# A fused attention and two-MLP kernel: every SBUF tile behind the constants moved up by 288 bytes

## The chip, the core and the metric

One core of one Trainium2 chip runs the whole kernel as a single program. The metric is device time in microseconds (us), the median of several runs. The profile is of one execution of the same program, with its own time.

## The reference

```
attention:  phi(x) = exp(x*scale @ omega.T - |x*scale|^2/2 - max) / sqrt(m)     q, k, v: [4, 8, 576, 64], 128 features
            out = phi(q) @ (phi(k).T @ v) / (phi(q) . sum(phi(k)) + 1e-6)       -> x [2304, 512]
first MLP:  h = x @ w_in [512, 2048];  g = h * sigmoid(1.702 h);  x = g @ w_out [2048, 512]
second MLP: 8 experts, one per token (argmax of x @ w_gate), weighted by the softmax of the gate:
            y = relu(x @ w1[e] [512, 1024]) @ w2[e] [1024, 512]
```

All inputs and outputs are float32.

## The kernel before

There are three stages, and TensorE works through them in one order that is written out by hand (no scheduler reorders anything).

**Attention** runs over 18 tiles of 128 tokens. Plain float32 matmuls project keys and queries (L228), sum keys against values (L254), transpose (L280, L305) and divide (L290). While it runs, VectorE and ScalarE decode the first MLP's weights and split each into a high part and a low part. The low parts go to DRAM (L155) and come back one 128x512 tile at a time (`wfetch` L369, `ofetch` L375).

**The first MLP** runs over five blocks of tokens, three of 512 and two of 384, and in each over 16 slices of 128 hidden features. For one block and slice, `hmm` (L436, L437, L438) makes 12 matmuls: for each of four contraction chunks high weight times high x, high weight times low x, low weight times high x. `gate` (L451 to L453) applies the gate and splits the result into `gh` and `gl`. `ymm` (L462, L463, L465) makes 12 matmuls more (9 in a block of 384). So a step is 24 matmuls of 512 columns, or 12 of 384 and 9 of 512. All operands are of type float32r, 4 bytes an element. Every matmul has a weight load (LDWEIGHTS) of its own, of a 128x128 operand, and TensorE loads the weights of the next matmul while the present one streams its moving operand.

**The second MLP** runs over 8 blocks of 288 gathered tokens of one expert each: `ffn1` (L802, L803, L806) and `ffn2` (L818, L819, L821), 12 matmuls of 288 columns each per 128 hidden features. The results are transposed back (L838) and scattered to DRAM (L845).

**Where the operands lie.** The tile framework places tiles in each SBUF partition from two sides. From the low side come the pools `keep` (its first tile is `cst`, the constants), `wts`, and the left pools of attention and of routing. From the top come the right pools `xa` and `xb`, which hold x's halves `xh` and `xl`, `gh`, `gl`, `sg` and one buffer of the second MLP's weights, `wh0`. The constants take 524 float32 a partition (2,096 bytes, L78), and what follows them starts where they end. The built program gives every tile's byte address. Modulo 512 they are, before the change:

| operands | role | address modulo 512 |
|---|---|---|
| `xh`, `xl` (right side) | moving in L436 to L438 | 480 |
| `win`, `l0` (left side) | weights in L436 to L438 | 192 |
| `wo`, `l1` (left side) | moving in L462, L463, L465 | 192 |
| `gh`, `gl` (right side) | weights in L462, L463, L465; moving in L818, L819, L821 | 480 |
| `yhl` (left side), chunk k = 0 to 3 | moving in L802, L803, L806 | 192, 320, 448, 64 |
| `wh0` (right side); `l0` (left side) | weights in L802, L803; in L806 | 480; 192 |
| `wh1`, `l1` (left side) | weights in L818 and L821; in L819 | 192 |
| `cst` (first tile of `keep`) | identity in the transposes | 128 |

So in the first MLP moving operand and weights lie 288 or 224 bytes apart modulo 512, that is, 224 bytes one way or the other. Where TensorE goes from one group to the next inside a step, two pairs agree: the weights `gh` of the first L462 are loaded while the last L438 streams `xh` (480 and 480), and the weights `win` of the next step's first L436 are loaded while the last L465 streams `wo` (192 and 192). In `ffn1` the four chunks of `yhl` lie at four addresses modulo 512: against `wh0` the distances are 224, 352, 480 and 96, against `l0` 0, 128, 256 and 384. In `ffn2` the distance is 288 throughout.

Of the kernel before, what the change touches and what calls it, by code (L numbers as in the profile page):

```python
# [10 lines left out]
F32 = mybir.dt.float32  # L11
# [37 lines left out]
NCONST = C_E8 + 8  # L49
# [21 lines left out]
def fused_kernel(ctx: ExitStack, tc: tile.TileContext, qT, kT, vt, omT, w_in, w_out, w_gate, w_gateT, w1, w2, consts, out):  # L71
    nc = tc.nc
    ctx.enter_context(tc.manual_schedule())
    keep = ctx.enter_context(tc.tile_pool(name="keep", bufs=1))
    drp = ctx.enter_context(tc.tile_pool(name="dr", bufs=1, space=DRAM))
    wts = ctx.enter_context(tc.tile_pool(name="wts", bufs=1))

    cst = keep.tile([128, NCONST], F32, name="cst")  # L78
    ident = cst[:, C_ID:C_ID + 128]
    xT = [keep.tile([128, KC, nb * 128], F32, name=f"big{i}", tag=f"big{i}") for i, (_, nb) in enumerate(BLOCKS)]  # L80
    win = [wts.tile([128, 4, KC, 128], F32R, name=f"win{i}", tag=f"win{i}") for i in range(4)]
# [234 lines left out]
    def advance():  # L316
        if ln[0] < len(seq):
            load(*seq[ln[0]])
        if 2 <= ln[0] < len(seq) + 2:
            square(*seq[ln[0] - 2])  # L320
        ln[0] += 1
# [13 lines left out]
    for t in range(3):  # L335
        if t >= 2:
            cload(1)
        advance()
    nc.sync.dma_start(out=cst, in_=consts)


    wg = []
# [345 lines left out]
    for n in range(len(steps) + 1):  # L688
        if n < len(steps):
# [52 lines left out]
            if (b, f) == (0, HF):  # L742
                assert cnext[4] == len(order)
                for i in range(2):
                    wg.append(keep.tile([128, 4, DM], F32, name=f"wg{i}", tag=f"wg{i}", bufs=1))
                    nc.sync.dma_start(out=wg[i].rearrange("p e d -> p (e d)"),
                                      in_=w_gate[4 * i:4 * i + 4].rearrange("(o e) d -> o (e d)", o=1).to_broadcast([128, 4 * DM]))
# [337 lines left out]
```

## Time and profile before

| | |
|---|---|
| median of 3 runs | 809.25 us (808.79 to 810.22) |
| the profiled execution's own time | 809.69 us |
| its span, first to last instruction | 807.9 us |
| TensorE matmul busy | 782.8 us, 97% of the span, 5681 instructions |
| VectorE, ScalarE, GpSimd busy | 483.5, 372.9 and 157.7 us |
| hardware DMA queue | 50.8% of 16 engines' span, 124.04 MB |

A busy share is the time in which at least one instruction of that engine was under way, divided by the span. Matmuls are pipelined: one of 512 columns is shown for 0.40 us, but the next one starts 0.23 us after it. What a matmul costs in a stream is therefore read from the starts of successive matmuls, not from their durations. The time outside the span (809.69 less 807.9) is 1.8 us.

### The profile page before, as it was taken

How to read it: one execution, taken by the hardware profiler on the slowest of the kernel's cores; microseconds unless marked ns; L12 is line 12 of the kernel's file. 1: busy time of each engine (PE TensorE's matmuls, PEld its weight loads, DVE VectorE, ACT ScalarE, POOL GpSimd, SP SyncE). 2: the span in 40 equal slices, each digit the busy share in tenths (PEclk: the TensorE clock that was granted, in tenths of full speed). 3: DMA queues.
4: the chain of work that ended last, by engine and by line, in shares of the span. 5: the costliest groups of instructions: out<-in, count | busy, mean ns of one | idle time of the engine just before them, and what ended most of it. 6: DMA issues, size and time to landing. Idle time of an engine off the chain costs nothing.

```text
span 807.9 us, 15072 instructions
## 1 busy us (share of the span) xinstructions
PE 782.8 (97%) x5681; PEld 700.5 (87%) x5681; DVE 483.5 (60%) x1075; ACT 372.9 (46%) x873; POOL 157.7 (20%) x129
## 2 busy tenths in 40 slices
PE   8999999799999999999999999999999999999994
PEld 7899998577888888888789988988999999999993
DVE  3688878679655137765315844744787556556551
ACT  5788889545433222212122123224454655555551
POOL 3656646100000111100020011100015502311011
PEclk9999999899999999999999999999999999999997
DMA  9877654389874473543335445974066646554011
GB/s 213 204 164 161 152 136 141 116 257 313 292 247 152 135 247 106 158 129 92 91 93 169 130 128 157 340 264 158 12 247 220 220 161 222 188 214 138 27 30 34
DMA packets 66016, 134.55 MB, mean 167 GB/s; under 512 B 24784, under 2 KB 24848, under 8 KB 61584
## 3 DMA queue, kind: packets, MB, share of 16 engines
q1 hardware_dynamic: 62784, 124.04, 50.8%
q0 software_dynamic: 3072, 9.44, 3.9%
q8 instruction: 47, 0.77, 0.4%
q14 instruction: 33, 0.27, 0.1%
q10 hardware_dynamic: 80, 0.03, 0.0%
HBM read 118.81 MB, written 18.87 MB: 170 GB/s over the span
## 4 chain that ended last, share of the span: by engine, by line
PE 58%; issue 23%; POOL 6%; DVE 5%; DMA 3%; ACT 2%; SPq 0%; POOLq 0%; ACTq 0%; DVEq 0%
PE py L462 8%; PE py L465 8%; PE py L463 8%; PE ph L436 7%; PE ph L437 7%; PE ph L438 7%; PE pj L228 6%; POOL out L845 2%; POOL yg L630 2%; PE kv L254 2%; PE nu L290 2%; PE tr L280 1%; DMA raw<-qT 1%; PE xt L305 1%; ACT phiq L237 1%
## 5 line engine op out<-in xcount | busy, mean ns | idle before, releaser
L451 ACT ACTIVATE gh<-ph 128x512 fp32r<-128x512 f32 (+1 forms) x80 | 44.5, 556 | 240.1 <-PE ph L438 240.1
L453 DVE TENSOR_TENSOR gl<-sg,gh 128x512 fp32r<-128x512 f32 (+1 forms) x80 | 51.1, 639 | 168.1 <-ACT sg L452 161.4
L438 PE MATMUL ph<-xh,l 128*128 128x512 f32 (+1 forms) x320 | 119.2, 373 | 1.0 <-DMA l<-lod 1.0
L436 PE MATMUL ph<-xh,win 128*128 128x512 f32 (+1 forms) x320 | 120.0, 375 | 0.0
L462 PE MATMUL py<-wo,gh 128*128 128x512 f32 x288 | 114.8, 399 | 4.6 <-ACT big L306 4.6
L437 PE MATMUL ph<-xl,win 128*128 128x512 f32 (+1 forms) x320 | 119.2, 372 | 0.2 <-DVE xl L178 0.2
L463 PE MATMUL py<-l,gh 128*128 128x512 f32 x288 | 114.8, 399 | 0.0
L497 DVE CUSTOM_DVE_ANT_0 junk<-ysb,wg 128x512 f32<-128x512 f32 x120 | 87.0, 725 | 3.1
L178 POOL TENSOR_TENSOR xl<-big,xh 128x512 fp32r<-128x512 f32 (+1 forms) x20 | 24.4, 1221 | 325.4 <-ACT xh L177 266.2
L465 PE MATMUL py<-wo,gl 128*128 128x512 f32 x288 | 81.0, 399 | 0.0
L228 PE MATMUL pj<-omx,raw 128*128 128x128 f32 x576 | 74.1, 284 | 2.1 <-DVE raw L213 1.5
L228 PEld LDWEIGHTS pj<-omx,raw 128*128 128x128 f32 x576 | 69.0, 197 | 4.4 <-issue 2.4
L213 POOL TENSOR_TENSOR raw<-raw 64x1024 f32<-64x1024 f32 (+1 forms) x34 | 65.0, 1916 | 37.1 <-DMA raw<-kT 14.2
L818 PE MATMUL oT<-gh,wh 128*128 128x288 f32 x256 | 72.1, 304 | 0.0
L802 PE MATMUL ph<-yhl,wh 128*128 128x288 f32 x256 | 72.0, 304 | 0.0
L819 PE MATMUL oT<-gh,l 128*128 128x288 f32 x256 | 70.1, 294 | 0.0
L803 PE MATMUL ph<-yhl,wh 128*128 128x288 f32 x256 | 69.9, 295 | 0.0
L437 PEld LDWEIGHTS ph<-xl,win 128*128 128x128 f32 x320 | 60.2, 188 | 10.5 <-DVE xl L178 0.6
L438 PEld LDWEIGHTS ph<-xh,l 128*128 128x128 f32 x320 | 60.1, 188 | 10.4 <-DMA l<-lod 1.9
L462 PEld LDWEIGHTS py<-wo,gh 128*128 128x128 f32 x288 | 54.6, 190 | 16.6 <-ACT big L306 4.9
L436 PEld LDWEIGHTS ph<-xh,win 128*128 128x128 f32 x320 | 60.2, 188 | 9.8
L235 DVE TENSOR_REDUCE nm<-pj 128x4 f32<-128x512 f32 x72 | 48.5, 688 | 30.6 <-PE pj L228 24.9
(178 smaller groups left out, 1437.9 us busy)
## 6 DMA issues: line engine op xcount, KB each, us to landing
l<-lod SPq DMA_DIRECT2D x160, 256.0 KB, 3.1
f<-w SPq DMA_DIRECT2D x20, 1024.0 KB, 6.3
e<-w SPq DMA_DIRECT2D x16, 1024.0 KB, 6.1
st<-w_in SPq DMA_DIRECT2D x16, 512.0 KB, 4.7
st<-w_out SPq DMA_DIRECT2D x16, 512.0 KB, 4.6
lod<-l SPq DMA_DIRECT2D x32, 256.0 KB, 3.5
yd<-ysb SPq DMA_DIRECT2D x22, 256.0 KB, 2.7
raw<-kT SPq DMA_DIRECT2D x18, 256.0 KB, 3.8
```

Of the source, the lines that this page charges most:

```text
L228: nc.tensor.matmul(p[:, j], r[:, 4 * g + j], omx, start=True, stop=True)
L436: nc.tensor.matmul(p, wh[:, c], xh, start=k == 0, stop=False)
L437: nc.tensor.matmul(p, wh[:, c], xl, start=False, stop=False)
L438: nc.tensor.matmul(p, wl[:, c], xh, start=False, stop=k == KC - 1)
L462: nc.tensor.matmul(p, gh[:, c], wh, start=(b, f) in pfirst, stop=False)
L463: nc.tensor.matmul(p, gh[:, c], wl, start=False, stop=False)
L465: nc.tensor.matmul(p, gl[:, j * 128:(j + 1) * 128], wh, start=False, stop=(b, f) in plast)
L497: nc.vector.tensor_tensor_reduce(out=junk, in0=ysb[b][j], in1=wg[e // 4][:, e % 4], scale=1.0, scalar=0.0, op0=ALU.mult, op1=ALU.add, accu ...
L802: nc.tensor.matmul(p, wh[:, w], yh[:, k], start=k == 0, stop=False)
L803: nc.tensor.matmul(p, wh[:, w], yl[:, k], start=False, stop=False)
L818: nc.tensor.matmul(p, wh[:, w], hh, start=f == 0, stop=False)
L819: nc.tensor.matmul(p, wl[:, w], hh, start=False, stop=False)
```

## The change

```diff
-    cst = keep.tile([128, NCONST], F32, name="cst")
+
+    cst = keep.tile([128, NCONST + 72], F32, name="cst")
...
-    nc.sync.dma_start(out=cst, in_=consts)
+    nc.sync.dma_start(out=cst[:, 0:NCONST], in_=consts)
```

The constants' tile gets 72 unused columns of 4 bytes, 288 bytes a partition. The tile itself stays where it is, and its load writes the same 2,096 bytes of each partition. Every tile that is placed from the low side behind it moves up by 288 bytes; the tiles of the right side stay. No instruction is added, removed or moved on any engine, and no wait or semaphore differs. Only addresses do (and, with the blank line, line numbers by one). Modulo 512, after the change:

| operands | address modulo 512 | distance, moving to weights |
|---|---|---|
| `xh`, `xl`, `gh`, `gl`, `win`, `l0`, `wo`, `l1` | 480 | 0 in L436 to L438 and in L462, L463, L465 |
| `yhl`, chunk k = 0 to 3 | 480, 96, 224, 352 | 0, 128, 256, 384 in L802, L803 and L806 |
| `wh1`, `l1` against `gh`, `gl` | 480 | 0 in L818, L819, L821 |
| operands of L228, L254 and L290 | as before to each other | as before |
| `cst` | 128 | differs by 288 against everything that it is used with from the low side |

288 is 4.5 times 64: tiles of the low side that began at a multiple of 64 bytes now begin 32 bytes past one.

## Rows read from the trace of the kernel before

**Rows 1.** The page: span, part 1 and the granted clock in 40 slices.
```profile
span 807.9 us, 15072 instructions
PE 782.8 (97%) x5681; PEld 700.5 (87%) x5681; DVE 483.5 (60%) x1075; ACT 372.9 (46%) x873; POOL 157.7 (20%) x129
PEclk9999999899999999999999999999999999999997
```
**Rows 2.** Busy time in the stages: first MLP, blocks of 512; of 384; the second MLP.
```profile
163.87:423.52 259.65, 258.45 (x1108) 206.71 (x1107) 143.53 (x308) 83.26 (x151) 14.82 (x12) 1.00 0.57 178
423.52:560.48 136.96, 136.96 (x706) 123.23 (x705) 76.43 (x231) 34.80 (x78) 7.85 (x8) 1.00 0.60 189
560.48:807.90 247.42, 233.38 (x1819) 230.83 (x1817) 145.49 (x318) 126.18 (x257) 51.33 (x48) 0.98 0.42 146
```
**Rows 3.** Waits of PE: waiter, released by: us in total, times, longest.
```profile
PE py L462 <- ACT big L306: 4.6, 1, 4.6
...
PE ph L438 <- DMA l<-lod: 1.0, 2, 0.8
```
**Rows 4.** Windows of PE alone: us, busy (matmuls touched), granted clock, DMA share, GB/s.
```profile
158.75:163.44 4.69, 4.69 (x12) 0.50 0.62 190
272.03:328.03 56.00, 56.00 (x241) 1.00 0.49 154
...
432.57:449.34 16.77, 16.77 (x85) 1.00 0.55 169
```
**Rows 5.** Lines by form: first-MLP and second-MLP matmuls, counts, durations of one.
```profile
L462 PE MATMUL py<-wo,gh 128*128 128x512 f32 x288 | 114.8, 399 | 4.6 <-ACT big L306 4.6
...
L436 PE MATMUL ph<-xh,win 128*128 128x512 f32 x192 | 76.2, 397 | 0.0
...
L818 PE MATMUL oT<-gh,wh 128*128 128x288 f32 x256 | 72.1, 304 | 0.0
...
L436 PE MATMUL ph<-xh,win 128*128 128x384 f32 x128 | 43.7, 342 | 0.0
```
**Rows 6.** Timeline of PE in one first-MLP step: start us, duration us, instruction.
```profile
274.60 0.39 PE L438 MATMUL ph<-xh,l 128*128 128x512 f32 x1
274.83 0.40 PE L462 MATMUL py<-wo,gh 128*128 128x512 f32 x1
275.06 0.40 PE L463 MATMUL py<-l,gh 128*128 128x512 f32 x1
...
277.39 0.40 PE L465 MATMUL py<-wo,gl 128*128 128x512 f32 x1
277.63 0.39 PE L436 MATMUL ph<-xh,win 128*128 128x512 f32 x1
277.86 0.40 PE L437 MATMUL ph<-xl,win 128*128 128x512 f32 x1
```
**Rows 7.** Timeline of PE in the second MLP: starts of an `ffn2` and an `ffn1` group.
```profile
655.40 0.29 PE L818 MATMUL oT<-gh,wh 128*128 128x288 f32 x1
...
657.00 0.30 PE L802 MATMUL ph<-yhl,wh 128*128 128x288 f32 x1
...
658.07 0.69 PE L806 MATMUL ph<-yhl,l 128*128 128x288 f32 x4
658.59 0.29 PE L818 MATMUL oT<-gh,wh 128*128 128x288 f32 x1
```
**Rows 8.** Lines L178 and L838: engine, operation, count, duration ns min/median/max, first and last start.
```profile
L178 DVE TENSOR_TENSOR l<-e,wh x64: 679/691/695, 555.7 to 759.7; 128x512 fp32r<-128x512 f32 x64
...
L838 PE MATMUL ob<-cst,oTs x96: 270/272/314, 617.1 to 796.2; 128*96 128x128 f32 x96
```
**Rows 9.** DMA issues: queue, count, KB each, median us from issue to landing.
```profile
raw<-kT SPq DMA_DIRECT2D x18, 256.0 KB, 3.8
v<-vt SPq DMA_DIRECT2D x18, 256.0 KB, 4.5
```
**Rows 10.** The chain that ended last: shares by engine.
```profile
PE 58%; issue 23%; POOL 6%; DVE 5%; DMA 3%; ACT 2%; SPq 0%; POOLq 0%; ACTq 0%; DVEq 0%
```

## The prediction

> **What bounds the kernel now.** I read the page first. TensorE is busy for 97% of the span, at the full clock in all but a few slices [rows 1], so first of all the time is what TensorE streams. The stage table says where this holds without a gap: in the first MLP's blocks of 512 it is busy for 258.45 of 259.65 us, in its blocks of 384 for all of 136.96, and in the second MLP for 233.38 of 247.42 [rows 2]. The reader should see that a nanosecond on each matmul of the first MLP is a nanosecond on the end, because nothing else ends last there: the longest waits of TensorE on others are one of 4.6 us on a ScalarE copy and 1.0 us in all on reloaded low weights [rows 3]. The chain of waits gives PE 58% and "issue" 23%, the latter mostly time behind TensorE's own pipelined stream; DMA has 3% [rows 10].
>
> Next I read what one matmul costs. Ten steps of 24 matmuls of 512 columns take 56.00 us, 240 starts after one another: 0.2333 us each [rows 4]. The same matmuls at half clock (granted clock 0.50) take 4.69 us for eleven, 0.4264 each [rows 4]. Half of that is 0.2132. So at full clock, and there alone, each matmul takes 0.0201 us more than its columns, some 9%. This excess is the only thing that an address could take away or add to, and the change is worth what it does to it.
>
> **The change part by part.** No instruction, wait or order changes on any engine, so nothing moves past anything else in a queue, and no new wait arises. Four kinds of address change are left.
>
> *Operands of the first MLP.* From 224 bytes apart modulo 512 to 0. The counts are 3 times 192 plus 3 times 288, so 1,440 matmuls of 512 columns, and 3 times 128, so 384 of 384 columns [rows 5]. How does TensorE do where the two agree already? Twice in each step they do. The last L438 streams from an address that agrees with the weights `gh` loaded meanwhile, and the next matmul starts 0.23 us later (274.60 to 274.83); the last L465 agrees with the next `win`, and the next starts 0.24 us later (277.39 to 277.63) [rows 6]. Together that is 0.47 us for two, where two ordinary ones take 0.4667. One is a little under the mean, one a little over, both within the rounding of the starts. From this I take 0 for the change. The two ends are every matmul at 0.23 or every one at 0.24. At 0.23: 1,440 times 0.0033 is 4.8 us, and 384 at three quarters of it 0.95, together a gain of 5.7 us. At 0.24: 1,440 times 0.0067 is 9.6 and 384 at three quarters 1.9, a loss of 11.5 us.
>
> Two more readings speak for 0. If the excess came from weight loads that collide with the stream, it would be one amount per matmul, since each loads the same 128x128 operand. Four steps of the blocks of 384 take 16.77 us [rows 4]; less 36 matmuls at 0.2333 (8.40) that leaves 8.37 for 48, 0.1744 each, against 0.1599 for the columns (three quarters of 0.2132): an excess of 0.0145, not 0.0201. In the second MLP twelve matmuls of 288 columns take 1.60 us in `ffn2` and 1.59 in `ffn1` [rows 7], so 0.1333 and 0.1325 against 0.1199: an excess of 0.013. It falls with the columns that are streamed, so most of it belongs to the stream itself and not to a meeting with the weights. Proportion would give 0.0113 at 288; what is over that, under 0.002 a matmul, is all that looks like a fixed piece per load.
>
> And `ffn1` is a trial of addresses made already: its chunks meet their weights at distances 0, 96, 128, 224, 256, 352, 384 and 480 modulo 512, `ffn2` at 288 alone. If the distance mattered, the two groups would differ by more than 1.59 against 1.60 [rows 7].
>
> The Trainium skill's page "TensorE: Matmul & The Clock Gate" (Part 2, "Step-by-step: what each phase is for") says that TensorE reads weights and moving operand through two independent SBUF ports, so that loading the next weights takes no read bandwidth from the running matmul. By it the change is worth 0 wherever the operands lie, and the two agreeing pairs of rows 6 go with it.
>
> *Operands of the second MLP.* `ffn2` goes from 288 to 0, `ffn1` from its eight distances to four (0, 128, 256, 384). 0 by the same reading; at the ends 768 matmuls of `ffn2` could gain the whole 0.0134 each, 10.3 us, which only the large rival below would bring, or lose in proportion to the first MLP's.
>
> *Transposes and attention.* The attention's matmuls keep their distances. The transposes use `cst`, which stays while the rest moves. L838 does so already with weights at four addresses modulo 512, and its shortest and median durations are 270 and 272 ns [rows 8]: 0.
>
> *VectorE, ScalarE, GpSimd and DMA.* Low-side tiles now start 32 bytes past a multiple of 64. VectorE's L178 reads its second operand alternately from `wh0` (480, such an address) and `wh1` (192, a multiple of 64), and all 64 last 679 to 695 ns [rows 8]: 0, and these engines have room. For DMA the trace shows no transfer of long rows to such an address. The nearest rows are the loads of k (rows of 4,096 bytes that begin on 64) with 3.8 us, and of v (pieces of 256 bytes every 260, most of which do not) with 4.5 us for the same 256 KB [rows 9], and that difference may be due to the short pieces alone. Lower end 0, since no start becomes a rounder one; upper end all DMA on the chain 18% longer: 3% of 807.9 is 24.2 us [rows 10], so 4.4 us. I take 0: in the MLPs TensorE waits on reloads for 1.0 us in all [rows 3], and what hides the rest is the matmul stream. If that cover went, L438 would be late first, on its low weights.
>
> **Sum.** 0 on the profiled execution's own time of 809.69 us, which is 0.44 above the median of 809.25. Carried to the median: **809.2 us**. The runs of before spread over 1.4 us, so about 0.2% is what can be told from no change.
>
> **The rivals.**
> 1. *The whole excess is a bank or line meeting of the two streams, and agreement removes it.* For it: the excess appears at full clock alone, as a limit of reading would. Against it: rows 6 and 7, where agreeing pairs and mixed distances show no gain. Price: 1,440 times 0.0201 is 28.9 us, and 384 times 0.0145 is 5.6; together 34.5, so about 775 us. `ffn2` would make it 765.
> 2. *A small part goes.* The agreeing L438 pair is the pattern (0.23), or the fixed piece under 0.002 us. Price 5.7 us at most: 803.5 us.
> 3. *Agreement costs.* When every weight load begins on the same line as the stream that it runs beside, the two meet at once in each matmul, and the L465 pair is the pattern (0.24 [rows 6]). It decides as soon as the mean start distance in a step exceeds 0.2345 us or so, 0.5% over now; at 0.24 it costs 11.5 us: 820.8 us. Against it: the other pair is under the mean, and the chunk at distance 0 in `ffn1` sits in the shorter group.
>
> That the change doesn't do what it says is no rival: the addresses in the built program are the stated ones.
>
> To rival 1, the same page (Part 1, "Wait — 56ns, not 53.3ns?") gives 512 columns at full clock as 512/2.4 plus 2.5 ns, 215.8 ns. The trace has 233.3 [rows 4]. By that figure 17.5 ns on 1,440 matmuls, 25.2 us, would be there to win, an estimate of 784 us; the page does not say what the rest is.
>
> **How the numbers follow.** No change 0.57, rival 1 0.11, rival 2 0.14, rival 3 0.18. So faster by over 0.2% 0.25, within it 0.57, slower 0.18. The range takes in the forecast, rival 2 to its end (803.5), the DMA bound (813.6) and the lower half of rival 3, to 815. Left out are rival 1 (0.11) and the upper half of rival 3 (0.09).
>
> **What would show it.** In the profile after, ten steps like those of rows 4 should again take 56.0 us, an `ffn2` group 1.60 and an `ffn1` group 1.59, and the PE row of the page should stay near 782.8 us. Rival 1 shows as steps of about 5.1 us in place of 5.60, rival 2 as 5.52, rival 3 as 5.64 to 5.76. A later start of the matmuls on low weights (the wait of L438 growing past a few us, or raw and l landing later) would show the DMA bound. The prediction is wrong if the steps differ from 5.60 by more than 0.02 us, or if a stage loses time in waits that rows 3 does not list.

## The result, and the profile after

| | before | changed |
|---|---|---|
| median | 809.44 us (808.79 to 810.22, 4 runs) | 802.31 us (800.25 to 803.71, 4 runs) |
| profiled execution, its span | 809.69, 807.9 us | 802.9, 801.0 us |
| TensorE matmul busy | 782.8 us | 774.5 us |

The ratio is 0.9909 [0.9885, 0.9934]: 7.1 us or 0.9% faster, more than the 0.2% that can be told from no change. The forecast was 809.2 us with no change likeliest; the time lies 1.2 us under the lower end of its range. Line numbers of the changed kernel are one higher, so L437 to L439 are the matmuls into `ph`, L463, L464 and L466 those into `py`.

The page of the changed kernel (span, part 1, granted clock), against [rows 1]:

```profile
span 801.0 us, 15072 instructions
PE 774.5 (97%) x5681; PEld 699.8 (87%) x5681; DVE 484.0 (60%) x1075; ACT 372.3 (46%) x873; POOL 157.8 (20%) x129
...
PEclk9999999999999999999999999999999999999997
```

The same instructions, the same granted clock but for one slice, the other engines' busy times unchanged within 0.6 us, and 8.3 us less matmul time. The waits of PE (waiter, releaser: us, times, longest) that [rows 3] names are there again:

```profile
PE py L463 <- ACT big L307: 4.6, 1, 4.6
...
PE ph L439 <- DMA l<-lod: 1.7, 2, 1.3
```

So neither wait went away; the one on low weights even grew by 0.7 us. The gain is in the stream itself. Windows of PE alone (us, busy with matmuls touched, clock, DMA share, GB/s) show it: ten steps of 24 matmuls of 512 columns, four steps in the blocks of 384, then the stages from the first `ph` matmul to the first one of 384 columns, from there to the second MLP, and the second MLP to its last L839. In the changed kernel:

```profile
275.85:330.25 54.40, 54.40 (x241) 1.00 0.50 165
426.68:443.42 16.74, 16.74 (x85) 1.00 0.56 167
146.78:417.62 270.84, 264.00 (x1183) 0.99 0.57 181
417.62:556.12 138.50, 138.50 (x713) 1.00 0.59 191
556.12:789.50 233.38, 231.00 (x1810) 0.99 0.43 149
```

And the same three stages before:

```profile
145.58:423.52 277.94, 271.97 (x1183) 0.99 0.57 176
423.52:562.30 138.78, 138.78 (x713) 1.00 0.60 191
562.30:796.20 233.90, 231.30 (x1811) 1.00 0.43 148
```

Ten steps take 54.40 us where they took 56.00 [rows 4], 5.440 a step for 5.600. That is 0.2267 a matmul for 0.2333, so each gained 0.0067 us, a third of the 0.0201 that each took beyond its columns. Were all 48 steps of the blocks of 512 to gain as much, it would be 48 times 0.160, 7.68 us. Their stage is 7.10 us shorter: busy time fell by 7.97 and time not busy rose by 0.87, of which 0.7 is the wait of L439. The blocks of 384, from which the prediction's bounds expected a third of any gain (0.95 us by their 384 matmuls of 384 columns and 0.95 by the 288 of 512 between them, of 5.7), are only 0.28 us shorter, and the second MLP 0.5 us. Up to the first `ph` matmul the profiled execution of the change lost 1.2 us (146.78 against 145.58). That is scatter: the further kernels below start there between 144.8 and 146.4, and the changed kernel, profiled again, at 145.3.

The timeline of PE in one step of the changed kernel (start us, duration us, instruction) is to be read beside [rows 6]:

```profile
273.13 0.39 PE L463 MATMUL py<-wo,gh 128*128 128x512 f32 x1
273.36 0.39 PE L464 MATMUL py<-l,gh 128*128 128x512 f32 x1
273.58 0.39 PE L463 MATMUL py<-wo,gh 128*128 128x512 f32 x1
...
274.94 1.07 PE L466 MATMUL py<-wo,gl 128*128 128x512 f32 x4
275.85 0.39 PE L437 MATMUL ph<-xh,win 128*128 128x512 f32 x1
```

The printed starts move by 0.23 and 0.22: a gap of 0.2267 and one of 0.2333 can both be printed as 0.23. Only a run of many matmuls tells the two apart.

### The profile page after: what moved, and what is told of

Read it like the earlier page. It is cut to its first block, busy times and chain, and to the rows that moved or that the text cites. A ratio compares the mean times of both kernels' runs of the same rounds, so it can differ in the third digit from the quotient of the medians.

```text
span 801.0 us, 15072 instructions
## 1 busy us (share of the span) xinstructions
PE 774.5 (97%) x5681; PEld 699.8 (87%) x5681; DVE 484.0 (60%) x1075; ACT 372.3 (46%) x873; POOL 157.8 (20%) x129
## 4 chain that ended last, share of the span: by engine, by line
PE 59%; issue 23%; POOL 6%; DVE 3%; DMA 3%; ACT 2%; SPq 1%; POOLq 0%; ACTq 0%; DVEq 0%
PE py L463 8%; PE py L464 8%; PE py L466 8%; PE ph L437 7%; PE ph L438 7%; PE ph L439 7%; PE pj L229 6%; POOL out L846 2%; POOL yg L631 2%; PE kv L255 2%; DMA lod<-l 2%; PE nu L291 2%; PE tr L281 1%; DMA raw<-kT 1%; PE xt L306 1%
## 5 line engine op out<-in xcount | busy, mean ns | idle before, releaser
L439 PE MATMUL ph<-xh,l 128*128 128x512 f32 (+1 forms) x320 | 118.1, 369 | 1.7 <-DMA l<-lod 1.7
L437 PE MATMUL ph<-xh,win 128*128 128x512 f32 (+1 forms) x320 | 118.8, 371 | 0.0
L438 PE MATMUL ph<-xl,win 128*128 128x512 f32 (+1 forms) x320 | 117.8, 368 | 0.3 <-DVE xl L179 0.3
L463 PE MATMUL py<-wo,gh 128*128 128x512 f32 x288 | 113.6, 394 | 4.6 <-ACT big L307 4.6
L464 PE MATMUL py<-l,gh 128*128 128x512 f32 x288 | 113.5, 394 | 0.0
L179 POOL TENSOR_TENSOR xl<-big,xh 128x512 fp32r<-128x512 f32 (+1 forms) x20 | 24.5, 1224 | 318.2 <-PE py L464 168.5
L466 PE MATMUL py<-wo,gl 128*128 128x512 f32 x288 | 78.9, 391 | 0.0
L803 PE MATMUL ph<-yhl,wh 128*128 128x288 f32 x256 | 72.1, 304 | 0.0
L819 PE MATMUL oT<-gh,wh 128*128 128x288 f32 x256 | 71.7, 303 | 0.0
L439 PEld LDWEIGHTS ph<-xh,l 128*128 128x128 f32 x320 | 60.0, 188 | 9.9 <-DMA l<-lod 2.6
L438 PEld LDWEIGHTS ph<-xl,win 128*128 128x128 f32 x320 | 60.1, 188 | 9.2 <-DVE xl L179 0.7
L463 PEld LDWEIGHTS py<-wo,gh 128*128 128x128 f32 x288 | 54.5, 189 | 15.4 <-ACT big L307 4.9
L437 PEld LDWEIGHTS ph<-xh,win 128*128 128x128 f32 x320 | 60.1, 188 | 8.5
```

Of the source, the lines that this page charges most:

```text
L437: nc.tensor.matmul(p, wh[:, c], xh, start=k == 0, stop=False)
L438: nc.tensor.matmul(p, wh[:, c], xl, start=False, stop=False)
L439: nc.tensor.matmul(p, wl[:, c], xh, start=False, stop=k == KC - 1)
L463: nc.tensor.matmul(p, gh[:, c], wh, start=(b, f) in pfirst, stop=False)
L464: nc.tensor.matmul(p, gh[:, c], wl, start=False, stop=False)
L466: nc.tensor.matmul(p, gl[:, j * 128:(j + 1) * 128], wh, start=False, stop=(b, f) in plast)
```

## The experiments

The theory after this comparison: how far the weights start behind the moving operand in the SBUF partition sets what each float32r matmul takes beyond its columns. The rivals: that it is where one of the two lies by itself, or what else the 288 bytes moved (constants, VectorE's and DMA's tiles, chance). Open as well were the period in bytes, what part of the excess can go, and why rows 6 and 7 had not shown it. A kernel's steps are judged by ten steps of its profile, its time by the ratio to runs of the kernel before on the same chip.

**Distances by themselves.** A small kernel with groups of 32 float32r matmuls in a row, each with its own weight load; it leaves out attention and both MLPs.

```diff
+ m0, w0 = (i % 4) * 512 + ms // 4, (i % 4) * 128 + wsx // 4
+ nc.tensor.matmul(p[:, 0:n], wei[:, w0:w0 + 128], mov[:, m0:m0 + n], ...)
```

> This kernel leaves out attention and both MLPs. It runs groups of 32 float32r matmuls, each with its own weight load, from one tile of moving data and one of weights, and each group keeps one start distance modulo 512 between the two. Theory A (the distance decides): the time from start to start depends on the distance; at 0 it is 0.2267 us for 512 columns, as after the change, at 224 about 0.2333, as before it, and two groups with the same distance at other addresses (256 against 256, 96 against 96) agree with distance 0. Theory B (the absolute address decides): groups follow the address modulo 64 or 512 of the moving operand or the weights, and 96 against 96 differs from 0 against 0. Theory C (neither; the difference is one of how the stream falls into step with its surroundings): all groups of 512 columns agree within 0.002 us.

Timeline of PE, one row a group. In a name the letters a to j stand for the digits 0 to 9; behind k is the start of the moving operand, behind w that of the weights, in bytes. The first three rows are 0/224, 0/256 and 0/288, the others 256/0, 96/96, 96/320 and, of 384 columns, 0/0:

```profile
73.51 7.63 PE L47 MATMUL mfbckaaawcce<-mov,wei 128*128 128x512 f32 x32
80.98 7.42 PE L47 MATMUL mfbckaaawcfg<-mov,wei 128*128 128x512 f32 x32
88.24 7.62 PE L47 MATMUL mfbckaaawcii<-mov,wei 128*128 128x512 f32 x32
...
177.26 7.42 PE L47 MATMUL mfbckcfgwaaa<-mov,wei 128*128 128x512 f32 x32
184.51 7.47 PE L47 MATMUL mfbckajgwajg<-mov,wei 128*128 128x512 f32 x32
191.82 7.63 PE L47 MATMUL mfbckajgwdca<-mov,wei 128*128 128x512 f32 x32
199.29 5.71 PE L47 MATMUL mdiekaaawaaa<-mov,wei 128*128 128x384 f32 x32
```

A group's cost is the next group's start less its own. At distance 224 that is 7.47 us (0.2334 a matmul), at 256 7.26 (0.2269). With the roles exchanged (256/0) it is 7.25. With both at 96 it is 7.31: the first nine gaps vary between 0.224 and 0.236, and the later ones settle, that is, repeat at 0.2267. With 96/320, again 224 apart, it is 7.47. So the distance decides and not the place of either operand, and the groups at 224 and 256 show the two values of the kernels, 0.2333 and 0.2267, with next to nothing else at work on the other engines. From 288 bytes on the values of 32 and so on came again: the period is 256 bytes and not 512.

**The other side moved.** The kernel before, with its right side moved down by 288 bytes and the constants' tile as it was. Moving operand and weights of the first MLP then agree, at 192 modulo 512.

```diff
+ rp = ctx.enter_context(tc.tile_pool(name="rp", bufs=1, side="right"))
+ rp.tile([128, 72], F32, name="rpad")
```

> The kernel before with 72 unused columns at the top of the right side, so that xh, xl, gh, gl, sg and wh0 move down by 288 bytes and the low side stays. All operands of the first MLP then lie at 192 modulo 512, a multiple of 64, and attention's tiles and the tiles that DMA fills on the low side are where they were. Theory A: steps of 24 matmuls take 5.44 us as after the change, the first MLP's three blocks of 512 gain about 7 us, and the first stage starts its matmuls at 145.6 us as before, so the whole is some 7 to 8 us faster than before. Theory B (the low side's new address gave the gain): steps stay at 5.60 us and the time at 809.

```profile
279.51:333.91 54.40, 54.40 (x241) 1.00 0.51 170
```

Ten steps in a window of PE alone take 54.40 us, as in the changed kernel. The median is 801.99 us, ratio 0.9897 [0.9882, 0.9912]. Neither the wider constants nor the low side's new addresses are needed; the distance is enough.

**Half of it.** Only the pool `xb` (`gh`, `gl`, `sg`, `wh0`) moves, so `ymm` and `ffn2` get distance 0 and `hmm` keeps 288.

```diff
+ xa.tile([128, 72], F32, name="xpad")
```

> The kernel before with gh, gl, sg and wh0 alone moved down by 288 bytes: L462, L463 and L465 get distance 0, L436 to L438 keep 288, ffn2 gets 0. Theory A: the twelve matmuls on y take 2.72 us and the twelve on h keep 2.80, steps 5.52 us, and the whole gains about half of the change's 7 us. Theory C: the gain comes only when the whole step agrees, so steps stay at 5.60 us.

The window of ten steps and then the timeline of PE, from the last L439 of a step through its `ymm`:

```profile
275.12:330.72 55.60, 55.60 (x241) 1.00 0.47 161
```

```profile
283.25 0.40 PE L439 MATMUL ph<-xh,l 128*128 128x512 f32 x1
283.49 0.40 PE L463 MATMUL py<-wo,gh 128*128 128x512 f32 x1
283.73 0.39 PE L464 MATMUL py<-l,gh 128*128 128x512 f32 x1
283.95 0.39 PE L463 MATMUL py<-wo,gh 128*128 128x512 f32 x1
284.18 0.40 PE L464 MATMUL py<-l,gh 128*128 128x512 f32 x1
284.42 0.39 PE L463 MATMUL py<-wo,gh 128*128 128x512 f32 x1
284.65 0.40 PE L464 MATMUL py<-l,gh 128*128 128x512 f32 x1
284.88 0.39 PE L463 MATMUL py<-wo,gh 128*128 128x512 f32 x1
285.11 0.39 PE L464 MATMUL py<-l,gh 128*128 128x512 f32 x1
285.34 1.07 PE L466 MATMUL py<-wo,gl 128*128 128x512 f32 x4
286.24 0.40 PE L437 MATMUL ph<-xh,win 128*128 128x512 f32 x1
```

The step is 5.56 us, a quarter of the way from 5.60 to 5.44 and not half. `hmm` keeps its 2.80 us for twelve matmuls, `ymm` takes 2.757 where twelve settled ones would take 2.72. The rows show where the rest stays: agreement begins with the L463 at 283.49, yet the gaps behind it are still 0.24, 0.22, 0.23, 0.24 and 0.23. From that L463 to the L466 at 285.34 eight matmuls take 1.85 us, 0.231 each; the last four take 0.90, 0.225 each. Every settled step of this run repeats that: by the trace's starts to the nanosecond the first seven gaps of `ymm` take 0.224 to 0.241 us and the later ones 0.227. So here the short gap is reached only after seven matmuls at the good distance. The number is not fixed: the group 96/96 of the small kernel took nine gaps to settle, while its group 0/256, which came after one at 224, held 0.2267 from its first matmul on. What decides it was not found. The median is 805.83 us, ratio 0.9943 [0.9927, 0.9958].

**256 in place of 512.** The constants 8 columns wider instead of 72 (the line is shown against the kernel before, the load is as in the change): the operands are 256 bytes apart modulo 512.

```diff
- cst = keep.tile([128, NCONST], F32, name="cst")
+ cst = keep.tile([128, NCONST + 8], F32, name="cst")
```

> The constants 8 columns wider, not 72: the low side moves up by 32 bytes, so that moving operands and weights of the first MLP lie 256 bytes apart modulo 512, and agree modulo 64 and 128. If agreement modulo 64, 128 or 256 is enough, steps take 5.44 us and the time is about 802 us as after the change. If the whole 512 count, steps stay near 5.60 us and the time near 809 us, or between.

```profile
279.22:333.62 54.40, 54.40 (x242) 1.00 0.49 169
```

Again 54.40 us for ten steps; 803.41 us (800.00 to 805.67), ratio 0.9921 [0.9901, 0.9941]. Agreement modulo 256 is enough, as in the small kernel. Here too the low side's tiles begin 32 bytes past a multiple of 64, as in the change.

**A scan.** The small kernel with 24 matmuls a group, at all 64 distances of whole elements within 256 bytes, with weights of 64 and 32 columns, with 384, 288 and 256 moving columns, and in bf16.

> This kernel leaves out attention and both MLPs and runs groups of 24 matmuls at one distance each, from the weights' start behind the moving operand's start, in steps of 4 bytes from 0 to 252 for 512 columns, in steps of 32 for 384, 288 and 256 columns, with weights of 64 and 32 columns, and in bfloat16. The run before showed that distances d and d + 256 give the same times. Theory A (the weights' read meets the stream's read in the same lines, and only the distance modulo 256 decides): at 512 columns the settled time is 0.2267 us at 0 and between that and 0.234 elsewhere, with no distance under 0.2267; narrower weights read less and leave a smaller excess, at 32 columns under half of the 0.020 us; in bfloat16, with half the bytes a column, the excess is nearly gone. Theory D (the excess belongs to the moving stream alone, as the prediction said): weights of 64 and 32 columns leave the time at 0.2267 to 0.2335.

Timeline of PE; the name gives type (r float32r, b bf16), moving columns, weight columns (n) and distance (w):

```profile
19.16 5.61 PE L54 MATMUL r512n128w0d<-mov,wei 128*128 128x512 f32 x24
24.60 5.74 PE L54 MATMUL r512n128w4d<-mov,wei 128*128 128x512 f32 x24
...
247.47 5.87 PE L54 MATMUL r512n128w164d<-mov,wei 128*128 128x512 f32 x24
253.18 5.76 PE L54 MATMUL r512n128w168d<-mov,wei 128*128 128x512 f32 x24
...
336.79 5.61 PE L54 MATMUL r512n128w228d<-mov,wei 128*128 128x512 f32 x24
342.24 5.71 PE L54 MATMUL r512n128w232d<-mov,wei 128*128 128x512 f32 x24
...
473.88 5.72 PE L54 MATMUL r512n32w0d<-mov,wei 128*32 128x512 f32 x24
479.44 5.87 PE L54 MATMUL r512n32w32d<-mov,wei 128*32 128x512 f32 x24
485.15 5.77 PE L54 MATMUL r512n32w224d<-mov,wei 128*32 128x512 f32 x24
...
495.95 5.34 PE L54 MATMUL b512n128w16d<-movb,weib 128*128 128x512 bf16 x24
501.13 5.34 PE L54 MATMUL b512n128w32d<-movb,weib 128*128 128x512 bf16 x23
```

From start to start over 24: 0.2267 at distance 0, 0.2271 at 228, 0.2379 at 164 (0.2387 once settled, the longest). Eight of the 64 distances settle at 0.2267 (0, 120, 132, 144, 156, 204, 228, 252), 30 at 0.2333, 20 between and six above; none settles below 0.2267. Theory A was met in that floor, but not in the six, which lie above its 0.234, and not in the narrow weights: weights of 32 columns, a quarter of the load, take no less, 0.2317 at 0 and 0.2379 at 32 (5.71 over 24). If the excess were time that the weight reads take from the stream, it should have shrunk. In bf16 a matmul takes 5.18 us over 24, 0.2158, and so at all five distances tried.

**A distance between.** The constants 24 columns wider: the weights start 64 bytes behind the moving operand in `hmm` and 192 in `ymm`, modulo 256.

```diff
+ cst = keep.tile([128, NCONST + 24], F32, name="cst")
```

> The constants 24 columns wider: the low side moves up by 96 bytes. The weights of L436 to L438 then lie 64 bytes behind their moving operand modulo 256, those of L462, L463 and L465 192 behind. By the run of single distances (Theory A) the twelve matmuls on h stay at 0.2334 us each, 2.80 in all, and the twelve on y settle near 0.2288, 2.75 in all or a little over: steps of some 5.55 to 5.58 us. If only agreement matters, both stay at 2.80.

```profile
277.21:333.01 55.80, 55.80 (x241) 1.00 0.47 161
```

Ten steps take 55.80 us, at the upper end of what was expected; one run, 808.12 us, where the median of the kernel before was 810.01 on that chip. This width, which brings no agreement, moves the time by little.

**The chunks of `ffn1`.** The other side moved, as above, and each chunk of `yhl` given 320 columns of space, so that all four begin at the same place modulo 256.

```diff
- yhl = wts.tile([128, 2, KC, BS], ...)
+ yhl = wts.tile([128, 2, KC, 320], ...)[:, :, :, 0:BS]
```

> The kernel with the right side moved down by 288 bytes, and yhl's chunks 320 columns apart in place of 288, so that the moving operands of ffn1 begin 1,280 bytes apart and all of its matmuls agree with their weights modulo 256. Theory A: ffn1 groups that nothing interrupts fall from 1.60 us to about 1.57 or 1.58, as those of ffn2 did, 64 groups times 0.015 to 0.02, so 1 us or so faster than with the right side moved alone; the steps of the first MLP stay at 5.44. If the excess of 288 columns is not one of distances, nothing changes.

Timeline of PE in the second MLP, an `ffn1` group, an `ffn2` group, and the next:

```profile
648.50 0.30 PE L804 MATMUL ph<-yhl,wh 128*128 128x288 f32 x1
...
650.08 0.30 PE L820 MATMUL oT<-gh,wh 128*128 128x288 f32 x1
...
651.66 0.30 PE L804 MATMUL ph<-yhl,wh 128*128 128x288 f32 x1
```

Both groups take 1.58 us, where `ffn1` took 1.60 in the changed kernel. But the total is the same, 802.33 us, ratio 0.9896 [0.9873, 0.9919]: the 1 us hoped for does not show, since with the right side moved alone 11 of the 27 `ffn1` groups that nothing interrupts were already at 1.57, and the stage is only 0.2 us shorter than there.

**The rhythm of the 384 blocks.** The small kernel, repeating 12 matmuls of 384 columns and 9 of 512, the first at each of 64 distances, the second at 0.

> This kernel leaves out attention and both MLPs and repeats the step of a block of 384, twelve matmuls of 384 columns and nine of 512, five times for each start distance of the 384 ones (0 to 252 by 4), with distance 0 for the 512 ones. At distance 0 it should repeat the 4.187 us a step of the changed kernel. If each group settles for itself, the best step is 12 times 0.1733 plus 9 times 0.2267, 4.120 us, at several distances. If a change of width always costs its several unsettled matmuls, no step is under some 4.16 us, as in the run where the matmuls on y alone agreed.

```profile
31.39 2.27 PE L44 MATMUL h0d0e<-mov,wei 128*128 128x384 f32 x12
33.50 2.24 PE L44 MATMUL y0d0e<-mov,wei 128*128 128x512 f32 x9
35.58 2.27 PE L44 MATMUL h0d0e<-mov,wei 128*128 128x384 f32 x12
```

At distance 0 a step takes 4.19 us (31.39 to 35.58), as in the changed kernel (16.74 over four), though settled matmuls would give 12 times 0.1733 and 9 times 0.2267, 4.12. The alternation of widths alone undoes the settling. Over all distances a step settles between 4.140 and 4.213 us. Neither of the two expectations for the best step is met: 4.12 is not reached, and ten distances lie under 4.16.

**The best distance for the 384 blocks.** The chunk version, with `xh` and `xl` in those blocks begun 112 bytes into their tiles, so that the weights are 144 behind.

```diff
- ...bufs=1)[:, 0:n] for m in "hl"]
+ ...bufs=1)[:, 512 - n and 28:(512 - n and 28) + n] for m in "hl"]
```

> The kernel with the right side moved and yhl's chunks 320 columns apart, and in the blocks of 384 columns xh and xl begin 28 columns (112 bytes) into their tiles, so that the weights of L436 to L438 lie 144 bytes behind them modulo 256; the run of mixed widths gave 4.140 us a step there against 4.187 at agreement. If the matmul stream alone decides, each of the 32 steps of those blocks loses 0.047 us, 1.5 us in all, and the time is that much under the kernel with the chunks moved, near 801 us. If other engines' reads and writes matter too, steps stay near 4.187.

```profile
428.82:445.49 16.67, 16.67 (x86) 1.00 0.41 125
```

Four steps take 16.67 us for 16.74, under half of what the small kernel promised, and the stage gains 0.6 us. The median is 802.19 us, ratio 0.9909 [0.9886, 0.9932]: no measurable gain over the changed kernel.

**The changed kernel again,** on the same chip as the last.

> The changed kernel itself, once more, on the same chip as the version that is meant to beat it: about 802 us again; its steps of 24 matmuls 5.440 us, and the start of the first MLP's matmuls anywhere between 145 and 147 us, since that is set by the first loads and not by the change.

802.05 us, ratio 0.9913 [0.9889, 0.9937]; its stage of 512 columns is 7.7 us shorter than before, the blocks of 384 0.3, the second MLP 0.5. The result repeats stage by stage. No version measured here is clearly faster than it.

## Why the prediction was wrong

**What bounds the kernel: right.** A nanosecond on each matmul of the first MLP was a nanosecond on the end: 1,152 matmuls by 0.0067 us are 7.7 us, and the blocks of 512 came out 7.1 and, profiled again, 7.7 us shorter.

**Operands of the first MLP: this is the step that failed,** in "From this I take 0". It took the two agreeing pairs of [rows 6] as samples of the state after. They are not. The pairs themselves were read rightly: in every settled step of the kernel before, the trace's starts to the nanosecond give 0.231 and 0.236 us for them, 0.467 together, as for two ordinary matmuls, so finer printing would not have helped. But where the whole step agrees, each matmul takes 0.2267. In the half version the shorter gap came only after seven matmuls in a row at the good distance; a single agreeing pair among 22 others can therefore keep the gap of its neighbours. There is a second reason that no run here separates from it: in those pairs a matmul agrees with the weights that are loaded beside it, not with its own, and in the settled steps that gained it agrees with both. The gain's end, 0.23 for every matmul or 5.7 us, was read off the rounding of the starts; the gap after the change lies under it, at 0.2267, and so the time fell out of the range.

**"If the distance mattered, the two groups would differ": failed too.** `ffn2` lay at 288, that is 32 modulo 256, and had 1.60 us. In the scan 288 columns settle at 0.1333 at the distances 32, 64, 96, 128 and 224 alike and at 0.1317 at 0, so twelve of them take 1.58 to 1.60 us at any mix of `ffn1`'s distances. The whole effect on a group is 0.02 us, and 1.59 against 1.60 lies inside it. When `ffn2` got distance 0 it went to 1.58, and when the chunks agreed `ffn1` did as well. Two groups at the same level proved nothing.

**"So most of it belongs to the stream itself": half right.** Most of the excess stays at every distance (0.0135 of 0.0201 us at the best), it does not shrink with narrower weights, and bf16 has nearly none (0.2158 against 0.2132 for the columns). But its premise, that the excess falls with the columns, was drawn from blocks of 384 that do not settle. Settled at their best distance in the scan, 512, 384 and 288 columns take 0.2267, 0.1733 and 0.1317 us, which is 0.0135, 0.0134 and 0.0118 more than their columns: what stays is closer to an amount per matmul than to a share of the columns. And the inference from there that an address does not matter was wrong: where the weights start sets a third of the excess.

**Rival 1 is refuted and rival 3 as stated too; rival 2 had the right sort and the wrong size.** Steps were named as the sign: 5.1 for rival 1, 5.52 for rival 2, 5.64 to 5.76 for rival 3. They are 5.44. A part of the excess goes, as in rival 2, but 0.0067 a matmul and not 0.0033. In exchange it goes only in the blocks of 512: the 0.95 us that were allotted to the matmuls of 384 columns, and the 288 matmuls of `ymm` between them, gave 0.28 us, because each change of width undoes the settling. Longer matmuls by address, as in rival 3, do exist (0.2387 at 164), but agreement is the best case and not the worst.

**The ports, and what there was to win.** Each settled matmul gained 0.0067 us by the distance alone. The Trainium skill ("TensorE: Matmul & The Clock Gate", Part 2, "Step-by-step: what each phase is for") says that weights and moving operand have independent read ports and that loading the next weights takes no read bandwidth from the running matmul. What the measurement overrules is the conclusion drawn from it, that the change is worth 0 wherever the operands lie: for float32r the spacing depends by 3% on how far apart they start. Whether the two reads meet anywhere no run here shows; in bf16 none of the five distances tried made a difference. The 215.8 ns of the same page of the Trainium skill (Part 1, "Wait — 56ns, not 53.3ns?") agrees with the 0.2158 us of bf16. The difference to 0.2267 goes with the type, and none of the 64 distances won any of it.

**The other terms: right at 0.** With tiles 32 bytes past multiples of 64, VectorE's L179 and the transposes L839 last what they did [rows 8]:

```profile
L179 DVE TENSOR_TENSOR l<-e,wh x64: 678/691/694, 549.7 to 753.3; 128x512 fp32r<-128x512 f32 x64
...
L839 PE MATMUL ob<-cst,oTs x96: 270/272/314, 611.6 to 789.5; 128*96 128x128 f32 x96
```

Of the DMA bound of 4.4 us only 0.7 us of wait on reloaded weights could be a trace, and the right-side version, which leaves the low side where it was, ends 0.3 us from the changed kernel. The second MLP was put at 0 and gained 0.5 us. The 64 groups of `ffn2` at 0.02 less should have given 1.3; where the rest of that went was not settled.

**What stays open.** Why the start of the weights acts on a stream of 4-byte elements, with a period of 256 bytes and with a memory of several matmuls, no run here shows; it is a measured dependence without a mechanism. Open too is whether a matmul's distance to its own weights counts or that to the weights loaded beside it, and what sets the number of matmuls until a group settles.

## What to carry to other kernels

In a kernel bound by long runs of float32r matmuls of one width, place moving tiles and weight tiles so that they start a multiple of 256 bytes apart in the partition; a pad of a few columns on either side of SBUF does it. Judge what a matmul costs by the starts of hundreds of them over a window; a pair in the middle of another rhythm need not show what a whole run at its distance costs, and gaps printed to 0.01 us hide a 3% effect. Where a kernel is 97% stream, a scan of the suspected quantity in a small kernel of its own says more than an inference from rows in which that quantity never stays constant.

## What the runs showed of the hardware that was not expected

- The distance of weights from moving operand acts modulo 256 bytes on float32r matmuls, with 0.2267 us for 512 columns at best (eight distances of 64) and 0.2387 at worst.
- The gap settles: in the half version seven matmuls in a row at the good distance were needed (0.231 each for the first eight, 0.225 for the last four), in the small kernel from none to nine, and a change of width at distance 0 starts it anew (4.19 us a mixed step for 4.12).
- Weights of 32 columns do not shorten the float32r stream (0.2379 at distance 32, where 128 columns settle at 0.2333).
- bf16 streams 512 columns in 0.2158 us at all five distances tried; float32r settles at none of 64 distances under 0.2267.
